# First heads, cap and constants loaded ahead of the branch; float64 conversion by 32-bit operations

## The chip, the core and the metric

The program runs on one core of a Trainium2 chip. Its engines are TensorE (PE, matmuls; PEld is its weight load), VectorE (DVE), ScalarE (ACT), GpSimd (POOL, unused here but for four memsets) and SyncE (SP), whose queue issues nearly all DMA transfers. The metric is device time in microseconds, the median of several runs.

## What is computed

Three layers, one after the other: attention with a soft cap, a feed-forward layer with a squared-ReLU-like function, and a second one with a maximum of three products. All tensors are float32 at the start; the weights reach the chip as float64 (see below).

```python
# 4 batches, 12 heads, 448 positions, head size 64; cap = 30
scores = q @ k.T / 8
scores = cap * tanh(scores / cap)
attn = exp(scores - max); attn /= attn.sum() + 1e-9
x = (attn @ v), heads side by side           # 1792 x 768
h = x @ w_in                                 # 768 -> 2048
g = where(h >= 1, h, where(h <= -1, 0, (h + 1)**2 / 4))
y = g @ w_out                                # 2048 -> 768
m = max(y @ w1, y @ w2, y @ w3)              # 768 -> 768, three times
out = m @ w_o2                               # 768 -> 768
```

## The kernel before

The entry (line 202) reads the cap's bits into a register on every engine and branches: above a limit it runs an arm that keeps the row maximum, otherwise (here) the arm without it. Each arm is the whole program, built by `softcap_attention_two_ffn` with its own pools.

**Work.** Activations lie transposed, channels on partitions, 448 positions of one batch along the free side. Batch 0 goes first: its attention, six pairs of heads, then the four matmul layers. Batch 1's attention is interleaved with batch 0's layers, batches 2 and 3's attention with batch 1's layers; the last two batches go through the layers together with a seven-product (Strassen) scheme. A matmul of the layers is three passes of float32r (a high and a low part of each operand), lines 863 to 865; the first six weight tiles (`PLAIN = 6`) are used as plain float32 matmuls, line 858, two passes of records each.

**Attention of a pair.** Two loads bring q and k of its two heads (`load_qk`, line 546), one brings v (549). Four chunks of keys: scores on TensorE (589 in batch 0, 578 later), tanh on ScalarE (596), exp (643). VectorE adds the four exps (281, tile `se`), TensorE sums over partitions with a tile of ones (672, 658), the sums go through memory to be inverted on few partitions (750, 771, 753, 758; the last pair inverts on VectorE at 782), and VectorE multiplies (281, tile `xf`) before the split into `x`.

**Weights.** On the first pass each weight tile, 128 partitions by 768 or 512 float64 numbers, is loaded into one of three `raw` buffers and turned into float32 in place, on the two 32-bit words of each number: the low word gives three rounding bits (`s0`, on VectorE at 410 or ScalarE at 408), the sign bit is put beside them (`sign`, 415, on VectorE), the high word is scaled as a float to move the exponent (`s1`, 422, ScalarE), and both are joined into the tile `wf` (`s3`, 426, VectorE), which is stored to memory for later passes. Before the change `s0` and `sign` write 16-bit quarters of the 64-bit number. There are 64 such tiles: 40 of 768, 24 of 512.

**Order.** Nothing is scheduled by the framework inside an arm. `Plan` gathers operations with a cost per engine, a due time (`want`) and the buffers that they take, plays them against each other at build time (`run`, line 65) and writes them out in the order of their planned starts; an operation with costs for two engines goes to the one that the plan finds free sooner. So a changed cost or dependency reorders the engines' instructions far from where it stands. On the chip each engine runs its list in order and waits on semaphores.

Of the kernel before, what the change touches and what calls it, by code (L numbers as in the profile page):

```python
# [10 lines left out]
I32 = mybir.dt.int32  # L11
U16 = mybir.dt.uint16
U32 = mybir.dt.uint32
BF16 = mybir.dt.bfloat16
# [9 lines left out]
class Plan:  # L24
# [29 lines left out]

    def op(self, cost, fn, want, deps=(), uses=(), takes=(), kind=None):
        o = Plan.Op()
        o.kind = kind
        o.cost, o.fn, o.want = cost, fn, want
        o.deps, o.takes = [d for d in deps if d is not None], list(takes)
        o.uses = list(dict.fromkeys([*uses, *takes]))  # L60
        for b in o.uses:
            b.users += 1
        for b in o.takes:
            self.order[b.pool].append((want, len(self.ops), b))
        o.n, o.out, o.t0, o.t1, o.e = 0, [], None, None, None
        self.ops.append(o)
        return o
# [133 lines left out]
def kernel(tc: tile.TileContext, qk, v, cap, *rest):  # L201


    bits = tc.nc.values_load(cap.bitcast(I32)[0:1, 0:1])
    with tc.If((bits & 0x7FFFFFFF) > LIMIT_BITS) as test:
        softcap_attention_two_ffn(tc, qk, v, cap, *rest, keep_max=True)
    with test.Else():
        softcap_attention_two_ffn(tc, qk, v, cap, *rest, keep_max=False)
# [3 lines left out]
def softcap_attention_two_ffn(  # L212
    ctx: ExitStack,
    tc: tile.TileContext,
    qk: bass.AP,
    v: bass.AP,
    cap: bass.AP,
# [34 lines left out]
    slots = {"u": 37, "h": 9, "v": 3, "w": 4, "wf": 4, "raw": 3, "rc": 2, "s": 2, "a": 1, "m": 3}  # L252
    const = pool("const", 1)
# [33 lines left out]
    def c_tt(n):  # L287
# [3 lines left out]


    ones = const.tile([C, D], F32, name="ones")
    nc.vector.memset(ones, 1.0)
    cap_sb = const.tile([P, 1], F32, name="cap_sb")
    nc.scalar.dma_start(out=cap_sb, in_=cap)

    nc.vector.scalar_tensor_tensor(
        out=cap_sb, in0=cap_sb, scalar=-1.0, in1=cap_sb, op0=ALU.mult, op1=ALU.max
    )  # L300
    qscale = const.tile([P, 1], F32, name="qscale")
    nc.vector.reciprocal(out=qscale, in_=cap_sb)
    nc.vector.tensor_scalar(
        out=qscale, in0=qscale, scalar1=1.0 / float(D) ** 0.5, scalar2=None, op0=ALU.mult
    )
# [79 lines left out]
    def fetch_first(i, want):  # L385
# [15 lines left out]
        def part(dtype, x):  # L401
            r = raw.tile.bitcast(dtype).rearrange("p (n four) -> p n four", four=4)
            return r[:, :n, x]

        def s0(e):
            lo, out_ = words()[0].bitcast(U32), part(U16, 0)
            if e == "A":
                nc.scalar.activation(out=out_, in_=lo, func=AF.Copy, scale=7.49 * 2.0**-32)  # L408
                return
            nc.vector.tensor_scalar(  # L410
                out=out_, in0=lo, scalar1=2.0**-29, scalar2=7.0, op0=ALU.mult, op1=ALU.min
            )

        def sign(e):
            nc.vector.tensor_scalar(  # L415
                out=part(U16, 1), in0=part(U16, 3), scalar1=0x8000, scalar2=None,
                op0=ALU.bitwise_and,
            )
# [20 lines left out]
        c = op({"D": 0.66 * k + 0.12}, sign, want - 17.7, [b], [raw])  # L439
# [88 lines left out]
    def attention(b, i, begin, last):  # L528
# [8 lines left out]
        qkt = [unit("qk")]  # L537
# [3 lines left out]

        def load_qk(e):
            for j in range(2):
                src = qk[b, 2 * i + j].rearrange("t p s -> p t s")
                o = slice(j * D, (j + 1) * D)
                nc.sync.dma_start(out=qkt[0].tile[o], in_=src[o])
# [6 lines left out]
        ql = op({"Q": 2.0}, load_qk, begin - (10 if full else 6), takes=qkt)  # L553
# [938 lines left out]
```

## Time and profile before

| | us |
|---|---|
| median of 3 runs | 996.36 (995.25 to 998.95) |
| profiled execution | 995.53 |
| its span, first to last instruction | 993.7 |
| TensorE busy | 963.0 (97%) |
| VectorE busy | 748.0 (75%) |
| ScalarE busy | 602.0 (61%) |
| DMA | 210.96 MB, mean 212 GB/s |

Busy times are sums over the whole span; the parts of the program have different limits, so they are read by stretches. Matmuls are pipelined and the profile models their ends, so small gaps between them do not show as idleness.

### The profile page before, as it was taken

The page shows a single profiled execution, that of the slowest core. Times are in us where ns is not written, and L with a number is a line of the kernel's source. Part 1 is how long each engine was busy: PE and PEld are TensorE (multiplying, and loading weights), DVE is VectorE, ACT ScalarE, POOL GpSimd, SP SyncE. Part 2 cuts the span into 40 slices and gives each one's busy share as a digit, 9 for nine tenths or more (in the row PEclk, how much of TensorE's full clock was granted, in tenths as well). Part 3 has the DMA queues.
Part 4 walks back from the last instruction along what each step waited for, and adds up shares of the span by engine and source line. Part 5 has one row for each costly group of instructions (what it writes and reads, how often), then busy time and mean ns, then how long its engine had stood idle before and what let it go on. Part 6 is the DMA issues. An engine that isn't in the chain of part 4 may idle for free.

```text
span 993.7 us, 14604 instructions
## 1 busy us (share of the span) xinstructions
PE 963.0 (97%) x5356; PEld 769.6 (77%) x5356; DVE 748.0 (75%) x1205; ACT 602.0 (61%) x876; POOL 0.2 (0%) x4
## 2 busy tenths in 40 slices
PE   5799999999999999999999999999999999999998
PEld 1124777877868877777777778999999999999997
DVE  1679999998989677877655667676898767858782
ACT  4788999787888478754445555555764524232431
POOL 0000000000000000000000000000000000000000
PEclk9799999999999999999999999999999999999999
DMA  5448877898898878688898765572364347437243
GB/s 127 150 147 261 264 230 226 266 292 274 289 293 270 293 248 277 224 283 286 289 319 275 228 209 188 166 238 80 129 200 139 107 147 235 136 103 238 88 147 131
DMA packets 111533, 210.96 MB, mean 212 GB/s; under 512 B 13022, under 2 KB 71518, under 8 KB 111454
## 3 DMA queue, kind: packets, MB, share of 16 engines
q1 hardware_dynamic: 109930, 209.87, 66.3%
q8 instruction: 44, 0.72, 0.3%
q10 hardware_dynamic: 1524, 0.08, 0.1%
q14 instruction: 35, 0.29, 0.1%
HBM read 142.90 MB, written 66.93 MB: 211 GB/s over the span
## 4 chain that ended last, share of the span: by engine, by line
PE 77%; ACT 9%; DVE 7%; DMA 4%; issue 2%; ACTq 0%; SPq 0%; DVEq 0%
PE ps_m L1263 21%; PE ps_s L1263 11%; PE ps_m L863 9%; PE ps_m L865 8%; PE ps_m L864 8%; PE ps_a L798 6%; PE ps_a L1263 5%; PE ps_s L578 4%; ACT raw L408 3%; PE ps_m L858 3%; DVE raw L415 2%; ACT t L643 2%; ACT raw L422 1%; DVE wf L426 1%; PE ps_s L589 1%
## 5 line engine op out<-in xcount | busy, mean ns | idle before, releaser
L1263 PE MATMUL ps_m<-op,w 128*128 128x448 f32 x1008 | 212.2, 368 | 0.0
L1263 PEld LDWEIGHTS ps_m<-op,w 128*128 128x128 f32 x1008 | 189.2, 188 | 19.1
L281 DVE TENSOR_TENSOR w<-wf,w 128x768 fp32r<-128x768 f32 (+1 forms) x146 | 120.6, 828 | 9.8 <-ACT w L276 8.0
L596 ACT ACTIVATE t<-ps_s,qscale 112x896 f32<-112x896 f32 x96 | 92.5, 1002 | 45.8 <-PE ps_s L578 39.2
L1263 PE MATMUL ps_s<-op,w 128*128 128x448 f32 x522 | 112.2, 368 | 0.0
L1263 PEld LDWEIGHTS ps_s<-op,w 128*128 128x128 f32 x522 | 98.0, 188 | 9.9
L643 ACT ACTIVATE t<-t,cap_sb 112x896 f32<-112x896 f32 x96 | 96.0, 1039 | 4.8 <-DVE rs L730 3.0
L276 ACT ACTIVATE w<-wf 128x768 fp32r<-128x768 f32 (+1 forms) x86 | 64.4, 750 | 55.9 <-PE ps_m L865 34.3
L798 PE MATMUL ps_a<-t,v 112*32 112x448 f32 (+1 forms) x752 | 82.8, 564 | 3.0 <-DVE xf L281 1.5
L863 PE MATMUL ps_m<-y,w 128*128 128x448 f32 x216 | 80.6, 373 | 0.0
L865 PE MATMUL ps_m<-y,w 128*128 128x448 f32 x216 | 79.2, 367 | 0.8 <-DVE w L281 0.8
L864 PE MATMUL ps_m<-y,w 128*128 128x448 f32 x216 | 79.0, 366 | 0.0
L278 DVE CAST w<-wf 128x512 fp32r<-128x512 f32 (+1 forms) x60 | 29.5, 492 | 57.3 <-PE ps_m L865 44.2
L863 PE MATMUL ps_m<-g,w 128*128 128x448 f32 x192 | 71.8, 374 | 0.0
L865 PE MATMUL ps_m<-g,w 128*128 128x448 f32 x192 | 70.5, 367 | 1.4 <-DVE w L281 1.4
L864 PE MATMUL ps_m<-g,w 128*128 128x448 f32 x192 | 70.3, 366 | 0.0
L422 ACT ACTIVATE raw<-raw 128x768 f32<-128x768 f32 (+1 forms) x64 | 53.6, 839 | 27.5 <-DVE raw L415 22.9
L415 DVE TENSOR_SCALAR raw<-raw 128x768 uint16<-128x768 uint16 (+1 forms) x64 | 60.1, 938 | 11.8 <-ACT raw L408 10.8
L408 ACT ACTIVATE raw<-raw 128x768 uint16<-128x768 uint32 (+1 forms) x37 | 62.9, 1700 | 2.2 <-DMA raw<-in_w_out 1.0
L281 DVE TENSOR_TENSOR w<-ss,w 128x384 fp32r<-128x384 f32 x80 | 43.7, 555 | 24.9 <-ACT w L276 22.8
L798 PEld LDWEIGHTS ps_a<-t,v 112*32 112x32 f32 (+1 forms) x752 | 24.2, 114 | 48.6 <-issue 32.8
L276 ACT ACTIVATE w<-ss 128x384 fp32r<-128x384 f32 x69 | 35.3, 520 | 40.8 <-PE ps_m L1263 21.0
(140 smaller groups left out, 1730.4 us busy)
## 6 DMA issues: line engine op xcount, KB each, us to landing
p<-w SPq DMA_DIRECT2D x60, 384.0 KB
w<-p SPq DMA_DIRECT2D x60, 384.0 KB
w<-wf SPq DMA_DIRECT2D x40, 384.0 KB
wf<-w SPq DMA_DIRECT2D x40, 384.0 KB
wf<-w SPq DMA_DIRECT2D x80, 192.0 KB
raw<-in_w SPq DMA_DIRECT2D x18, 768.0 KB
raw<-in_w_in SPq DMA_DIRECT2D x16, 768.0 KB
raw<-in_w_out SPq DMA_DIRECT2D x24, 512.0 KB
```

The source lines that it names most:

```text
L276: nc.scalar.activation(out=out_, in_=in_, func=AF.Copy)
L281: nc.vector.tensor_tensor(out=out_, in0=a, in1=b, op=o)
L408: nc.scalar.activation(out=out_, in_=lo, func=AF.Copy, scale=7.49 * 2.0**-32)
L415: nc.vector.tensor_scalar(out=part(U16, 1), in0=part(U16, 3), scalar1=0x8000, scalar2=None, op0=ALU.bitwise_and,)
L422: nc.scalar.activation(out=hi, in_=hi, func=AF.Copy, scale=2.0**-112)
L596: nc.scalar.activation(out=t[c].tile, in_=ps.tile[:C, :, :S], func=AF.Tanh, scale=qscale[:C])
L643: lambda e, c=c: nc.scalar.activation(out=t[c].tile, in_=t[c].tile, func=AF.Exp, scale=cap_sb[:C]),
L798: nc.tensor.matmul(pa.tile[j * D + d : j * D + d + n, :S], vt.tile[:, j, c, d : d + n], t[c].tile[:, j], start=start, stop=stop,)
L863: nc.tensor.matmul(ps.tile[:, :S], wh, a.tile[:, 0], start=start, stop=False)
L864: nc.tensor.matmul(ps.tile[:, :S], wh, a.tile[:, 1], start=False, stop=False)
L865: nc.tensor.matmul(ps.tile[:, :S], wl, a.tile[:, 0], start=False, stop=stop)
L1263: nc.tensor.matmul(get(), w_, x_, start=start and z == 0, stop=stop and z == 2, skip_group_check=begun,)
```

## The change

Ahead of the branch the entry now opens a pool, loads the first pair's q and k into a tile of its own (`qk0`), loads the cap, fills the ones, and works out the cap's absolute value and the scale of the scores; both arms use them. The first pair's scores then depend on no planned load. The pool of `u` buffers has 36 instead of 37 slots. In the conversion `s0` writes the whole low word as a 32-bit integer, and `sign` takes the sign bit from the high word and joins it to the low word in one operation with two inputs, at a planned cost of 1.05 instead of 0.66 us per 1000 columns.

```diff
+    def fixed(self, tile_):
+        b = Plan.Buf(None, None)
+        b.tile = tile_
+        return b
...
-        o.uses = list(dict.fromkeys([*uses, *takes]))
+        o.uses = [b for b in dict.fromkeys([*uses, *takes]) if b.pool]
...
-def tile_softcap_attention_two_ffn_kernel(tc: tile.TileContext, qk, v, cap, *rest):
-    bits = tc.nc.values_load(cap.bitcast(I32)[0:1, 0:1])
+@with_exitstack
+def tile_softcap_attention_two_ffn_kernel(
+    ctx: ExitStack, tc: tile.TileContext, qk, v, cap, *rest
+):
+
+
+    nc = tc.nc
+    bits = nc.values_load(cap.bitcast(I32)[0:1, 0:1])
+    const = ctx.enter_context(tc.tile_pool(name="const", bufs=1))
+    qk0 = const.tile([128, 2, qk.shape[4]], F32, name="qk0")
+    load_heads(nc, qk0, qk, 0, 0)
+    cap_sb = const.tile([128, 1], F32, name="cap_sb")
+    nc.scalar.dma_start(out=cap_sb, in_=cap)
+    ones = const.tile([v.shape[2], 64], F32, name="ones")
+    nc.vector.memset(ones, 1.0)
+    nc.vector.scalar_tensor_tensor(
+        out=cap_sb, in0=cap_sb, scalar=-1.0, in1=cap_sb, op0=ALU.mult, op1=ALU.max
+    )
+    qscale = const.tile([128, 1], F32, name="qscale")
+    nc.vector.reciprocal(out=qscale, in_=cap_sb)
+    nc.vector.tensor_scalar(
+        out=qscale, in0=qscale, scalar1=0.125, scalar2=None, op0=ALU.mult
+    )
+    consts = const, qk0, cap_sb, ones, qscale
     with tc.If((bits & 0x7FFFFFFF) > LIMIT_BITS) as test:
-        softcap_attention_two_ffn(tc, qk, v, cap, *rest, keep_max=True)
+        softcap_attention_two_ffn(tc, consts, qk, v, *rest, keep_max=True)
     with test.Else():
-        softcap_attention_two_ffn(tc, qk, v, cap, *rest, keep_max=False)
+        softcap_attention_two_ffn(tc, consts, qk, v, *rest, keep_max=False)
+
+
+def load_heads(nc, to, qk, b, i):
+    D = qk.shape[3] // 2
+    for j in range(2):
+        src = qk[b, 2 * i + j].rearrange("t p s -> p t s")
+        o = slice(j * D, (j + 1) * D)
+        nc.sync.dma_start(out=to[o], in_=src[o])
...
-    slots = {"u": 37, "h": 9, "v": 3, "w": 4, "wf": 4, "raw": 3, "rc": 2, "s": 2, "a": 1, "m": 3}
-    const = pool("const", 1)
+    slots = {"u": 36, "h": 9, "v": 3, "w": 4, "wf": 4, "raw": 3, "rc": 2, "s": 2, "a": 1, "m": 3}
+    const, qk0, cap_sb, ones, qscale = consts
...
-    ones = const.tile([C, D], F32, name="ones")
-    nc.vector.memset(ones, 1.0)
-    cap_sb = const.tile([P, 1], F32, name="cap_sb")
-    nc.scalar.dma_start(out=cap_sb, in_=cap)
-    nc.vector.scalar_tensor_tensor(
-        out=cap_sb, in0=cap_sb, scalar=-1.0, in1=cap_sb, op0=ALU.mult, op1=ALU.max
-    )
-    qscale = const.tile([P, 1], F32, name="qscale")
-    nc.vector.reciprocal(out=qscale, in_=cap_sb)
-    nc.vector.tensor_scalar(
-        out=qscale, in0=qscale, scalar1=1.0 / float(D) ** 0.5, scalar2=None, op0=ALU.mult
-    )
...
         def s0(e):
-            lo, out_ = words()[0].bitcast(U32), part(U16, 0)
+            lo = words()[0]
             if e == "A":
-                nc.scalar.activation(out=out_, in_=lo, func=AF.Copy, scale=7.49 * 2.0**-32)
+                nc.scalar.activation(
+                    out=lo, in_=lo.bitcast(U32), func=AF.Copy, scale=7.49 * 2.0**-32
+                )
                 return
             nc.vector.tensor_scalar(
-                out=out_, in0=lo, scalar1=2.0**-29, scalar2=7.0, op0=ALU.mult, op1=ALU.min
+                out=lo, in0=lo.bitcast(U32), scalar1=2.0**-29, scalar2=7.0,
+                op0=ALU.mult, op1=ALU.min,
             )
 
         def sign(e):
-            nc.vector.tensor_scalar(
-                out=part(U16, 1), in0=part(U16, 3), scalar1=0x8000, scalar2=None,
-                op0=ALU.bitwise_and,
+            lo, hi = words()
+            nc.vector.scalar_tensor_tensor(
+                out=lo, in0=hi, scalar=-(2**31), in1=lo, op0=ALU.bitwise_and,
+                op1=ALU.bitwise_or,
             )
...
-        c = op({"D": 0.66 * k + 0.12}, sign, want - 17.7, [b], [raw])
+        c = op({"D": 1.05 * k + 0.15}, sign, want - 17.7, [b], [raw])
...
-        qkt = [unit("qk")]
+        early = first and i == 0
+        qkt = [plan.fixed(qk0) if early else unit("qk")]
...
-        def load_qk(e):
-            for j in range(2):
-                src = qk[b, 2 * i + j].rearrange("t p s -> p t s")
-                o = slice(j * D, (j + 1) * D)
-                nc.sync.dma_start(out=qkt[0].tile[o], in_=src[o])
...
-        ql = op({"Q": 2.0}, load_qk, begin - (10 if full else 6), takes=qkt)
+        ql = None if early else op(
+            {"Q": 2.0}, lambda e: load_heads(nc, qkt[0].tile, qk, b, i),
+            begin - (10 if full else 6), takes=qkt,
+        )
```

**SyncE at the program's start**, through the branch to the first loads of the arm. Before:

```order
L1488 UNCONDITIONAL_BRANCH
L204 TENSOR_LOAD in_cap_ptr
L204 TENSOR_LOAD in_cap
L205 REGISTER_ALU
L205 COMPARE_AND_BRANCH
L546 DMA qk<-in_qk 64x2x448 x2
L549 DMA v<-in_v 112x2x256
L546 DMA qk<-in_qk 64x2x448 x2
```

Now:

```order
L1502 UNCONDITIONAL_BRANCH
L239 DMA qk_65<-in_qk 64x2x448 x2
L211 TENSOR_LOAD in_cap_ptr
L211 TENSOR_LOAD in_cap
L228 REGISTER_ALU
L228 COMPARE_AND_BRANCH
L560 DMA v<-in_v 112x2x256
L239 DMA qk<-in_qk 64x2x448 x2
```

The two loads of the first heads (`qk`, now `qk_65`) moved from behind the branch to the head of the queue; what follows the branch stands as it did, without them.

**VectorE in the first pairs' attention**, from behind the sum of the first pair on; `rs<-ps_r` is such a sum, `rc` is the inversion of a pair's sums, `xf` the product with them, `raw` the conversion of weights. Before:

```order
L281 TENSOR_TENSOR se<-t 112x896
L281 TENSOR_TENSOR se<-se,t 112x896
L771 RECIPROCAL rc<-rc 56x16
L281 TENSOR_TENSOR se<-se,t 112x896
L730 TENSOR_SCALAR rs<-ps_r,eps_sb 128x224
L410 TENSOR_SCALAR raw<-raw 128x768
L415 TENSOR_SCALAR raw<-raw 128x768
L281 TENSOR_TENSOR se<-t 112x896
L281 TENSOR_TENSOR se<-se,t 112x896
L771 RECIPROCAL rc<-rc 56x16
L410 TENSOR_SCALAR raw<-raw 128x768
L281 TENSOR_TENSOR xf<-ps_a,rs 128x448
```

Now:

```order
L312 TENSOR_TENSOR se<-t 112x896
L785 RECIPROCAL rc<-rc 56x16
L312 TENSOR_TENSOR se<-se,t 112x896 x2
L744 TENSOR_SCALAR rs<-ps_r,eps_sb 128x224
L312 TENSOR_TENSOR se<-t 112x896
L312 TENSOR_TENSOR xf<-ps_a,rs 128x448
L312 TENSOR_TENSOR se<-se,t 112x896
L309 CAST x<-xf 128x448
L312 TENSOR_TENSOR x<-xf,x 128x448
L785 RECIPROCAL rc<-rc 56x16
L312 TENSOR_TENSOR se<-se,t 112x896
```

The first `xf` moved ahead of all conversion and of the second pair's `rc`; it stood behind three conversion steps and that `rc`.

**VectorE at the end of batch 0's attention**, from the last pair's first sum on; `wf` are the joined weights that the plain matmuls read, `rs` with x4 the last pair's inversion. Before:

```order
L281 TENSOR_TENSOR se<-t 112x896
L281 TENSOR_TENSOR xf<-ps_a,rs 128x448
L426 SCALAR_TENSOR_TENSOR wf<-raw 128x768
L278 CAST x<-xf 128x448
L281 TENSOR_TENSOR x<-xf,x 128x448
L771 RECIPROCAL rc<-rc 56x16
L281 TENSOR_TENSOR se<-se,t 112x896 x2
L426 SCALAR_TENSOR_TENSOR wf<-raw 128x768 x2
L281 TENSOR_TENSOR qk_lo<-qk,qk_hi 128x896
L782 RECIPROCAL rs<-rs 128x112 x4
L281 TENSOR_TENSOR xf<-ps_a,rs 128x448
```

Now:

```order
L312 TENSOR_TENSOR se<-t 112x896
L312 TENSOR_TENSOR se<-se,t 112x896
L785 RECIPROCAL rc<-rc 56x16
L312 TENSOR_TENSOR se<-se,t 112x896
L312 TENSOR_TENSOR xf<-ps_a,rs 128x448
L442 SCALAR_TENSOR_TENSOR wf<-raw 128x768
L309 CAST x<-xf 128x448
L312 TENSOR_TENSOR x<-xf,x 128x448
L796 RECIPROCAL rs<-rs 128x112 x4
L312 TENSOR_TENSOR xf<-ps_a,rs 128x448
L442 SCALAR_TENSOR_TENSOR wf<-raw 128x768
L312 TENSOR_TENSOR x<-xf,x 128x448
```

Here the second of the four first `wf` stood ahead of the last sums, with one more much earlier; now the first of them stands behind the last sum, and the second behind the four reciprocals. (In the same place the three exponent steps of ScalarE, line 422, now 438, stand behind its last exp.)

## Rows read from the trace of the kernel before

**Rows 1.** Three stretches: us, busy PE PEld DVE ACT POOL, granted clock, DMA share, GB/s

```profile
25.00:50.00 25.00, 19.11 (x160) 4.60 (x160) 15.85 (x22) 17.57 (x19) 0.00 (x0) 0.80 0.48 149
81.00:330.00 249.00, 241.93 (x1327) 188.36 (x1327) 232.84 (x335) 212.85 (x264) 0.00 (x0) 1.00 0.86 267
330.00:600.00 270.00, 270.00 (x1675) 212.82 (x1675) 181.89 (x276) 159.56 (x215) 0.00 (x0) 1.00 0.80 263
```

**Rows 2.** Chain of waits, 0 to 50 us: start us, us, what

```profile
0.72 0.86 SPq L204
...
2.24 2.53 issue
4.77 6.23 DMA qk<-in_qk
...
41.41 0.45 DVE xf L281
```

**Rows 3.** Timeline of the start: start us, us, engine line operation [idle before]

```profile
4.77 3.17 SPq L546 DMA_DIRECT2D qk<-in_qk  x2
...
11.52 1.28 ACT L325 ACT_TABLE_LOAD   x1 [11.52 <-DVE cap_sb L298]
...
14.06 1.01 ACT L596 ACTIVATE t<-ps_s,qscale 112x896 f32<-112x896 f32 x1 [1.05 <-PE ps_s L589]
...
19.36 1.09 DVE L281 TENSOR_TENSOR se<-t 112x896 f32<-112x896 f32 x1 [6.16 <-ACT t L643]
```

**Rows 4.** Timeline of ScalarE, later in batch 0's attention

```profile
47.00 0.93 ACT L422 ACTIVATE raw<-raw 128x768 f32<-128x768 f32 x1 [3.66 <-DVE rs L730]
...
67.19 1.26 ACT L422 ACTIVATE raw<-raw 128x768 f32<-128x768 f32 x1
...
71.34 1.04 ACT L643 ACTIVATE t<-t,cap_sb 112x896 f32<-112x896 f32 x1
```

**Rows 5.** Timeline of VectorE, end of batch 0's attention

```profile
69.73 0.39 DVE L278 CAST x<-xf 128x448 fp32r<-128x448 f32 x1
...
76.21 2.99 DVE L782 RECIPROCAL rs<-rs 128x112 f32<-128x112 f32 x4
...
79.30 0.62 DVE L281 TENSOR_TENSOR xf<-ps_a,rs 128x448 f32<-128x448 f32 x1
```

**Rows 6.** Chain of waits, where the plain matmuls begin

```profile
77.25 1.41 PE ps_s L578 x12
...
81.00 22.75 PE ps_m L858 x60
```

**Rows 7.** Conversion steps by line and shape: xcount | busy, mean ns | idle before

```profile
L415 DVE TENSOR_SCALAR raw<-raw 128x768 uint16<-128x768 uint16 x40 | 41.9, 1048 | 7.5 <-ACT raw L408 7.0
L408 ACT ACTIVATE raw<-raw 128x768 uint16<-128x768 uint32 x21 | 41.1, 1955 | 1.1 <-ACT rs L728 0.6 <-DMA raw<-in_w 0.5
...
L426 DVE SCALAR_TENSOR_TENSOR wf<-raw 128x768 int32<-128x768 int32 x40 | 38.4, 963 | 1.5 <-ACT raw L422 1.5
L422 ACT ACTIVATE raw<-raw 128x768 f32<-128x768 f32 x40 | 37.2, 932 | 20.5 <-DVE raw L415 16.6 <-DVE rs L730 3.7
...
L408 ACT ACTIVATE raw<-raw 128x512 uint16<-128x512 uint32 x16 | 21.9, 1366 | 1.1 <-DMA raw<-in_w_out 1.0
...
L410 DVE TENSOR_SCALAR raw<-raw 128x768 uint16<-128x768 uint32 x19 | 19.9, 1046 | 0.3 <-DMA raw<-in_w_in 0.3
...
L422 ACT ACTIVATE raw<-raw 128x512 f32<-128x512 f32 x24 | 16.4, 683 | 7.0 <-DVE raw L415 6.3 <-ACT t L596 0.5
```

**Rows 8.** Waits from 81 to 330 us: total us, times, longest

```profile
ACT raw L422 <- DVE raw L415: 22.9, 32, 2.2
...
PE ps_m L865 <- DVE w L281: 2.2, 4, 0.8
```

**Rows 9.** SyncE's queue: two of the loads of raw weight tiles

```profile
76.71 0.43 SPq L399 DMA_DIRECT2D raw<-in_w_in  x1
...
106.69 0.33 SPq L399 DMA_DIRECT2D raw<-in_w_in  x1
```

More of the change, by code (lines that the diff above doesn't have):

```diff
@@ L11 @@
 I32 = mybir.dt.int32
-U16 = mybir.dt.uint16
 U32 = mybir.dt.uint32
-BF16 = mybir.dt.bfloat16
 I64 = mybir.dt.int64
@@ L198, in emit, with kernel @@
             o.fn(o.e)
-def kernel(tc: tile.TileContext, qk, v, cap, *rest):
-    bits = tc.nc.values_load(cap.bitcast(I32)[0:1, 0:1])
+@with_exitstack
+def kernel(
+    ctx: ExitStack, tc: tile.TileContext, qk, v, cap, *rest
[18 more added lines that the diff above has]
+    consts = const, qk0, cap_sb, ones, qscale
     with tc.If((bits & 0x7FFFFFFF) > LIMIT_BITS) as test:
-        softcap_attention_two_ffn(tc, qk, v, cap, *rest, keep_max=True)
+        softcap_attention_two_ffn(tc, consts, qk, v, *rest, keep_max=True)
     with test.Else():
-        softcap_attention_two_ffn(tc, qk, v, cap, *rest, keep_max=False)
+        softcap_attention_two_ffn(tc, consts, qk, v, *rest, keep_max=False)
[5 more added lines that the diff above has]
+        nc.sync.dma_start(out=to[o], in_=src[o])
 @with_exitstack
@@ L214, in softcap_attention_two_ffn @@
     tc: tile.TileContext,
+    consts,
     qk: bass.AP,
     v: bass.AP,
-    cap: bass.AP,
     w_in: bass.AP,
@@ L399, in load @@
             nc.sync.dma_start(out=raw.tile[:, :n], in_=units[i])
-        def part(dtype, x):
-            r = raw.tile.bitcast(dtype).rearrange("p (n four) -> p n four", four=4)
-            return r[:, :n, x]
         def s0(e):
-            lo, out_ = words()[0].bitcast(U32), part(U16, 0)
+            lo = words()[0]
             if e == "A":
-                nc.scalar.activation(out=out_, in_=lo, func=AF.Copy, scale=7.49 * 2.0**-32)
+                nc.scalar.activation(
+                    out=lo, in_=lo.bitcast(U32), func=AF.Copy, scale=7.49 * 2.0**-32
+                )
                 return
             nc.vector.tensor_scalar(
-                out=out_, in0=lo, scalar1=2.0**-29, scalar2=7.0, op0=ALU.mult, op1=ALU.min
+                out=lo, in0=lo.bitcast(U32), scalar1=2.0**-29, scalar2=7.0,
+                op0=ALU.mult, op1=ALU.min,
             )
         def sign(e):
-            nc.vector.tensor_scalar(
-                out=part(U16, 1), in0=part(U16, 3), scalar1=0x8000, scalar2=None,
-                op0=ALU.bitwise_and,
+            lo, hi = words()
+            nc.vector.scalar_tensor_tensor(
+                out=lo, in0=hi, scalar=-(2**31), in1=lo, op0=ALU.bitwise_and,
+                op1=ALU.bitwise_or,
             )
```

## The prediction

> **What bounds the kernel now.** I read the stretches first, then the chain of waits, and last the timelines of the places where TensorE stands. TensorE is busy in nearly all of the span, so the question is where it is not. From 330 to 600 us it is busy all of the time [rows 1], and after the first pass over the weights the built order of its matmuls is the same in both programs but for a few that change places; nothing that this change does can be worth much there. Two places are left. The **head**, 0 to 81 us, is the first batch's attention: TensorE works 19.1 us of the 25 between 25 and 50, at a granted clock of 0.80 [rows 1], because tanh and exp on ScalarE are the slower side. The **first pass over the weights**, 81 to 330 us, has TensorE idle for only 7.07 us of 249, beside a VectorE at 232.8 us (94%), a ScalarE at 212.9 us (85%) and transfers at 0.86 [rows 1]. All four are near their limit there, and the float64 conversion that the change touches runs only in that stretch and at the end of the head. So the most that I see is 7 us in the stretch, some more that pipelined ends hide, and what the head gives.
>
> **The loads outside of the arms.** SyncE spends 0.72 to 2.24 us on reading the cap and branching, then 2.53 us until its first instruction in the arm, and only at 4.77 us issues the first heads, which land at 11.00 [rows 2]. In the new order that issue stands ahead of the reading, so it moves to 0.72: 4.05 us earlier, with landing near 6.95. The reading and the branch now follow the two issues, which take 3.17 us of SyncE's queue [rows 3]: 0.72 + 3.17, and then the same 4.05 us to the arm, make 7.94, just when SyncE was through with the first heads before (4.77 + 3.17). So everything behind them in that queue, the second pair's heads first, is issued when it was; nothing of it is earlier. The cap constants: ScalarE's issue moves up by the same step; before, the table load that waits for the cap ran from 11.52 to 12.80 and the first tanh started at 14.06 [rows 3]. Shifted, the load ends at 8.75, the first tanh can start at 10.0, and the scores are last there, as before. VectorE now waits for the cap (until about 7.5) ahead of its branch; behind that wait stand its own reading and branch, 4.05 us more on SyncE, and its first sum, at 19.36 before [rows 3], is not due before 15. I take 4.05 us for the first tanh; bounds 2.5, were the issue no earlier than the old branch at 2.24, and 4.8, were it at the span's start.
>
> **The head, reordered.** The planner's order of the head is new, and this counts for more than the shift. Before, VectorE did a low-word step, a sign step and the wait for the second reciprocal ahead of the first product with the reciprocal, xf; it came at 41.41, and the chain of waits runs through it to TensorE [rows 2]. In the new order xf stands ahead of all conversion. Before, ScalarE did two exponent steps (L422, 0.93 and 1.26 us) between the tanhs, one of them after 3.66 us of idleness; the last exp ended at 72.38 [rows 4]. In the new order all three exponent steps stand behind the last exp. So the last exp comes 4.05 + 2.2 = 6.2 us earlier, at 66.1. Bounds: 68.3 where only the shift is left, 62.4 where the 3.66 of idleness goes too [rows 4].
>
> But what stood between the tanhs now stands behind them. From the last exp VectorE has in row: sum 1.09, xf 0.62, first weights 0.95, cast 0.39, difference 0.62, four reciprocals 2.99, xf 0.62, second weights 0.95, difference 0.62, third weights 0.95, xf 0.62: 10.4 us (durations of [rows 3, 5, 7]; a difference is taken as xf, the same shape). TensorE can start the plain matmuls 2.8 us after the exp, does four, stands 1.6 us for the xf behind the reciprocals, and has 13 done at 14.4 us after the last exp, none of the next batch's 24 scores. A plain one takes 0.755 us here (30 in 22.75 us, two records each) [rows 6]. Before, 8.6 us after the last exp (81.0) it had 6 done and the 24 scores, which are 2.8 us at 1.41 for twelve [rows 6]. Seven plain ones more are 5.3 us, so the new order is where the old one was at 14.4 - 5.3 + 2.8 = 11.9 us instead of 8.6: **3.3 us given back**. The head is then 6.2 - 3.3 = 2.9 us ahead; bounds 6.6 ahead (last exp at 62.4) and 0.8 (68.3).
>
> **The 32-bit steps.** By the built order the low-word step goes to ScalarE 26 times wide and 19 narrow (before 21 and 16), to VectorE 14 and 5 (before 19 and 8). The step on ScalarE takes 1955 ns wide and 1366 narrow; the exponent step, the same engine and shape with the same stride, 32 bits in and out, takes 932 and 683 [rows 7]. Nothing in the trace parts the 16-bit output from the reading of unsigned integers. I take the output as the cause: the ratio holds for both widths, so the cost is by the element, and VectorE's two 16-bit forms (1046 and 1048) are both slower than its 32-bit form with two inputs (963) [rows 7]. With that, ScalarE goes from 62.9 to 26 x 0.932 + 19 x 0.683 = 37.2 us, **25.7 us less**; at the old price it would be 76.8, 13.9 more. Those are the bounds. The Trainium skill, "ScalarE: Activation LUTs", section "What ACT_TABLE_LOAD costs", gives 186 ns + 0.833 ns an element for an activation with immediate scale, for fp32 and bf16 alike: an estimate of 826 ns wide. By that rule a 2-byte output costs nothing, the excess would lie in something that the change keeps, and the change would add work to ScalarE; the trace disagrees with its number already (932, 1955), and no run shown tells which half of it fails.
>
> VectorE: the sign step becomes the form of L426, 963 for 1048 ns, 40 times, and narrow ones likewise: 5 us less. The low-word step, 8 fewer: 7.5 us less at 1046 ns. Together **12.5 us less** of 232.8. The page "VectorE: DVE Perf Modes" of the Trainium skill, section "What auto-detection actually checks", lets a one-source operation in SBUF run two elements a cycle; the 16-bit step at 1046 ns does not show it. If the 32-bit step did, another 8 us or so would go.
>
> In the stretch a raw tile comes back every third load: 76.71 to 106.69 is six loads, 5.0 us each [rows 9]. The largest wait there is inside the conversion, 22.9 us of ScalarE for the sign step [rows 8]. Taking about 1.0 us out of a tile's way on ScalarE, and 38 us of work off the two engines that TensorE waits for (2.2 us for weights' low parts alone [rows 8]), should free all of the 7.07 us that TensorE stands. I take 7.1; bounds 0 and 10, where the hidden gaps go as well. What is late next is TensorE itself. The tile qk0 costs one of 37 slots for the whole program; after 330 us TensorE has no idle time in which this would show, so I take nothing.
>
> **Sum.** The profiled execution took 995.53 us (span 993.7 and 1.8 around it). 995.5 - 2.9 - 7.1 = 985.5. The median of the runs shown is 0.83 above that execution, so 986.3.
>
> **Rivals.**
> *More of it goes.* The last exp at 62.4 and the hidden gaps too: 995.5 - 6.6 - 10 + 0.8 = 979.7. For it: the idle pieces of ScalarE in the head stand where the order is new. Against it: the queue of reciprocals through memory stays.
> *The low-word step keeps its price on ScalarE*, since reading unsigned integers is what costs. Then ScalarE gains 13.9 us of work in a stretch where it is at 85%, VectorE is rid of 12.5, and the two cancel: 995.5 - 2.9 + 0.8 = 993.4, from 990 to 999. By the ScalarE page of the Trainium skill, as told above, it would be this one.
> *Weights come too late (slower).* No raw tile comes back before the last exp, so the fourth load, issued before while the attention ran, waits until then. Where the last exp comes at 68.3, the head gains 0.8 us, but the stream of weights is one tile behind, 5.0 us [rows 9], and TensorE stands in front of the plain matmuls; if its granted clock then falls as it did between 25 and 50 (0.80 in the mean, so 10 of the 25 us at 1.2 GHz instead of 2.4 [rows 1]), that is 5.0 more: 995.5 - 0.8 + 5 + 5 + 0.8 = 1005.5. It decides from a last exp at 69.1 on (72.4 - 3.3), where the head has nothing left to pay for it, and only if the stretch gains nothing.
>
> **How the numbers follow.** Chances: the forecast 0.55, more of it 0.18, the old price 0.18, late weights 0.09. A measurement of this kernel tells about 0.5% (5 us) from no change, so faster means under 991.4. The forecast's own spread (981 to 993) lies under that about nine times in ten; with the first rival, and a quarter of the second, that makes 0.72 faster; 0.19 the same; 0.09 slower. The range goes from 979 to 997: it leaves out the slow rival, the far end of the second and a little of the first.
>
> **What would show it.** Right: the first heads issued at about 0.7 us and the first tanh near 10; the last exp near 66, the last plain matmul near 101, as against 103.75; the low-word step on ScalarE near 0.93 us, the sign step near 0.96; TensorE idle under 2 us between 81 and 330. Wrong: a low-word step still near 1.9 us; a last exp at 68 or later; TensorE standing for first weights after the attention, at a lower granted clock.

## The result, and the profile after

The changed kernel takes 982.65 us in the median of four runs (980.67 to 983.78), the kernel before 995.81 beside it: a ratio of 0.9865, 95% interval 0.983 to 0.9899. The forecast was 986.3, from 979 to 997. The profiled execution took 983.78 us with a span of 982.0, 11.7 less than before.

Four stretches of the kernel after, with the columns of [rows 1]:

```profile
25.00:50.00 25.00, 21.78 (x184) 4.89 (x176) 16.72 (x25) 19.53 (x21) 0.00 (x0) 0.86 0.53 172
130.00:140.00 10.00, 8.01 (x32) 6.91 (x31) 10.00 (x16) 9.94 (x17) 0.00 (x0) 0.83 0.71 221
81.00:330.00 249.00, 247.01 (x1378) 198.92 (x1379) 220.15 (x325) 193.48 (x277) 0.00 (x0) 0.99 0.89 280
330.00:600.00 270.00, 270.00 (x1678) 212.76 (x1677) 186.09 (x282) 165.54 (x222) 0.00 (x0) 1.00 0.80 259
```

TensorE's idle time between 81 and 330 us fell from 7.07 to 1.99 us, all of it between 130 and 140, where the granted clock also is 0.83 in the mean. VectorE and ScalarE are 12.7 and 19.4 us less busy there.

The chain of waits of the kernel after, the start and the plain matmuls (against [rows 2, 6]):

```profile
0.73 3.58 DMA qk<-in_qk
4.31 2.87 issue
7.17 3.31 PE ps_s L603 x12
...
71.35 7.21 PE ps_m L872 x18
...
82.33 16.73 PE ps_m L872 x44
```

The heads are there at 4.31 us, at 11.00 before. What is last for the first scores is no longer a transfer but 2.87 us in which TensorE waits for nothing that the profile shows; I take them for its way into the arm. The last plain matmul ends at 82.33 + 16.73 = 99.06, at 103.75 before. Behind that matmul TensorE has the same work left in both programs: the same 508 matmuls lie up to it in the traces of all kernels of this study, among themselves differently arranged. So the 11.7 us split cleanly: **4.7 ahead of it, and 7.0 behind it** (993.7 - 103.75 = 889.95 before; 982.0 - 99.06 = 882.94 after).

The start and the end of the first attention in the timeline of the kernel after (against [rows 3, 4]):

```profile
0.73 1.42 SPq L239 DMA_DIRECT2D qk<-in_qk  x2
...
6.08 1.28 ACT L341 ACT_TABLE_LOAD   x1 [6.08 <-issue]
...
9.01 1.01 ACT L610 ACTIVATE t<-ps_s,qscale 112x896 f32<-112x896 f32 x1 [1.43 <-PE ps_s L603]
...
14.30 1.09 DVE L312 TENSOR_TENSOR se<-t 112x896 f32<-112x896 f32 x1 [6.38 <-ACT t L657]
...
63.14 1.04 ACT L657 ACTIVATE t<-t,cap_sb 112x896 f32<-112x896 f32 x1
64.08 2.52 ACT L438 ACTIVATE raw<-raw 128x768 f32<-128x768 f32 x3
...
66.76 3.27 PE L872 MATMUL ps_m<-xf,wf 128*128 128x448 f32 x8 [0.34 <-DVE wf L442]
71.35 7.21 PE L872 MATMUL ps_m<-xf,wf 128*128 128x448 f32 x18 [1.32 <-DVE xf L312]
```

The conversion steps of the kernel after by line and shape (against [rows 7]; L420 and L424 are the low-word step, L431 the sign step):

```profile
L431 DVE SCALAR_TENSOR_TENSOR raw<-raw 128x768 int32<-128x768 int32 x40 | 38.4, 961 | 7.0 <-ACT raw L420 6.6
...
L420 ACT ACTIVATE raw<-raw 128x768 int32<-128x768 uint32 x26 | 23.8, 914 | 6.9 <-DMA raw<-in_w 4.5 <-DMA raw<-in_w_in 1.8 <-ACT rs L742 0.6
...
L420 ACT ACTIVATE raw<-raw 128x512 int32<-128x512 uint32 x19 | 12.8, 672 | 2.6 <-DMA raw<-in_w_out 2.6
...
L424 DVE TENSOR_SCALAR raw<-raw 128x768 int32<-128x768 uint32 x14 | 8.1, 578 | 0.4 <-DMA raw<-in_w 0.2
```

The step on ScalarE still reads unsigned integers and writes 32 bits: 914 for 1955 ns, 672 for 1366. On VectorE it fell too, from 1046 to 578. The waits from 81 to 330 us of the kernel after (against [rows 8]):

```profile
ACT raw L438 <- DVE raw L431: 5.1, 9, 1.6
ACT raw L420 <- DMA raw<-in_w: 4.5, 6, 1.3
...
PE ps_m L877 <- ACT h L307: 2.0, 1, 2.0
```

The wait inside the conversion is down from 22.9 us to 5.1; ScalarE now waits for weights to land, and TensorE waits once, 2.0 us, for an eviction.

### The profile page after: what moved, and what is told of

Same layout as the page of the kernel before. It is cut to its first block, busy times and chain, and to the rows that moved or that the text cites. A ratio compares the mean times of both kernels' runs of the same rounds, so it can differ in the third digit from the quotient of the medians.

```text
span 982.0 us, 14606 instructions
## 1 busy us (share of the span) xinstructions
PE 959.8 (98%) x5356; PEld 771.0 (79%) x5356; DVE 730.1 (74%) x1191; ACT 582.8 (59%) x890; POOL 0.2 (0%) x4
## 4 chain that ended last, share of the span: by engine, by line
PE 94%; ACT 4%; DVE 1%; issue 1%; DMA 0%; ACTq 0%; DVEq 0%
PE ps_m L1277 21%; PE ps_m L877 14%; PE ps_m L878 13%; PE ps_m L879 13%; PE ps_s L1277 11%; PE ps_a L812 7%; PE ps_s L592 5%; PE ps_a L1277 5%; PE ps_m L872 3%; ACT t L657 2%; PE ps_r L686 1%; PE ps_s L603 1%; ACT t L610 1%; DMA qk<-in_qk 0%; DVE rs L796 0%
## 5 line engine op out<-in xcount | busy, mean ns | idle before, releaser
L307 ACT ACTIVATE w<-wf 128x768 fp32r<-128x768 f32 (+1 forms) x90 | 67.2, 747 | 57.4 <-PE ps_m L879 31.5
L309 DVE CAST w<-wf 128x512 fp32r<-128x512 f32 (+1 forms) x56 | 27.0, 482 | 60.2 <-PE ps_m L879 43.8
L877 PE MATMUL ps_m<-x,w 128*128 128x448 f32 x156 | 59.3, 380 | 2.0 <-ACT h L307 2.0
L431 DVE SCALAR_TENSOR_TENSOR raw<-raw 128x768 int32<-128x768 int32 (+1 forms) x64 | 54.9, 858 | 7.9 <-ACT raw L420 7.5
L878 PE MATMUL ps_m<-x,w 128*128 128x448 f32 x156 | 57.6, 370 | 0.0
```

Source lines behind the costliest of these rows:

```text
L307: nc.scalar.activation(out=out_, in_=in_, func=AF.Copy)
L431: nc.vector.scalar_tensor_tensor(out=lo, in0=hi, scalar=-(2**31), in1=lo, op0=ALU.bitwise_and, op1=ALU.bitwise_or,)
L877: nc.tensor.matmul(ps.tile[:, :S], wh, a.tile[:, 0], start=start, stop=False)
L878: nc.tensor.matmul(ps.tile[:, :S], wh, a.tile[:, 1], start=False, stop=False)
```

## Experiments

For each kernel the table gives the timed median, the ratio to the runs of before on the same chip, and from its trace the end of the last plain matmul and what was left of the span behind it. The last two columns come from one execution each. The kernels ran on several chips, on which before has medians from 994.89 to 996.73, so medians of different chips are to be compared by the ratio. loads_only, bits_only, order_kept_16 and sign_16 share one chip; shift_only, bits_old_cost, act32_dve16 and dve32_act16 a second; loads_old_cost and v_banks_old a third; v_banks and exp_dve a fourth.

| kernel | median us | ratio, 95% interval | last plain ends | behind it |
|---|---|---|---|---|
| before | 995.81 | | 103.75 | 889.95 |
| after | 982.65 | 0.9865 (0.983 to 0.9899) | 99.06 | 882.94 |
| loads_only | 992.19 | 0.9963 (0.9947 to 0.9978) | 98.64 | 890.8 |
| bits_only | 988.36 | 0.9911 (0.9884 to 0.9939) | 103.83 | 882.9 |
| bits_old_cost | 984.80 | 0.9888 (0.9868 to 0.9907) | 105.82 | 880.0 |
| order_kept_16 | 986.81 | 0.9893 (0.9862 to 0.9923) | 99.90 | 890.9 |
| act32_dve16 | 983.87 | 0.9884 (0.9864 to 0.9904) | 96.44 | 882.9 |
| dve32_act16 | 986.86 | 0.9919 (0.9901 to 0.9937) | 98.44 | 879.5 |
| sign_16 | 982.02 | 0.986 (0.9836 to 0.9884) | 96.50 | 882.7 |
| shift_only | 984.81 | 0.9888 (0.9866 to 0.991) | 100.26 | 883.0 |
| loads_old_cost | 982.95 | 0.9868 (0.9837 to 0.9899) | 99.95 | 882.2 |
| v_banks | 979.45 | 0.983 (0.9806 to 0.9855) | 94.17 | 881.0 |
| v_banks_old | 979.70 | 0.9826 (0.9801 to 0.9851) | 96.84 | 879.5 |
| exp_dve | 976.17 | 0.9798 (0.978 to 0.9817) | 94.65 | 878.8 |

### One part of the change at a time

loads_only is the kernel after with the steps of before:

```
-            lo = words()[0]
+            lo, out_ = words()[0].bitcast(U32), part(U16, 0)
...
-        c = op({"D": 1.05 * k + 0.15}, sign, want - 17.7, [b], [raw])
+        c = op({"D": 0.66 * k + 0.12}, sign, want - 17.7, [b], [raw])
```

> The kernel before with the first heads, the cap and the constants loaded ahead of the branch (36 slots of u), the conversion left with its 16-bit forms. Theory (two gains that add): the head gains what it gained in the kernel after, last exp near 64 us and last plain matmul near 99 to 100, while TensorE still stands for about 7 us between 81 and 330 us: 995.8 - 4.7 = 991. Rival (the head's lead is eaten by the stretch, since the weights arrive no sooner): last plain matmul near 99, but more idle time of TensorE behind it, 995 to 996. Second rival (the stretch stands only because the head is late): 984.

bits_only is the kernel before with the changed steps, the mirror of that diff, and the loads inside the arms.

> The kernel before with the low-word and sign steps in 32 bits and the planner's new cost for the sign step, all loads inside the arms (37 slots of u). Theory: head as before (first tanh near 14.1, last exp near 72), low-word step on ScalarE 0.91 us and on VectorE 0.58 us, TensorE idle under 2.5 us between 81 and 330 us: 995.8 - 7 = 989, from 987 to 991. Rival (the gain of the stretch needs the earlier head): 994 to 996.

Both came as the first theory said: loads_only moves the last plain matmul to 98.64 and leaves 890.8 us behind it (TensorE stands for 9.4 us between 81 and 330, where about 7 were expected); bits_only leaves it at 103.83 and has 882.9 behind it. The parts add, to within the scatter: 3.7 us and 7.6 us by the medians, 11.3 together, and 13.2 for both.

### Price or order

The steps' forms change their price, and the planner's new cost of the sign step changes the order. bits_old_cost has the new forms in the order of before, word for word on TensorE and SyncE:

```
-        c = op({"D": 1.05 * k + 0.15}, sign, want - 17.7, [b], [raw])
+        c = op({"D": 0.66 * k + 0.12}, sign, want - 17.7, [b], [raw])
```

> The kernel before with the low-word and sign steps in 32 bits and nothing else: the planner keeps the old costs, so that the order of every engine is that of before, and the low-word step stays with the engine that had it (ScalarE 21 wide and 16 narrow, VectorE 19 and 8). Theory (the price of the step frees the stretch): from the last plain matmul (near 104) to the end 883 us as in bits_only, not 890 as before: 988 to 989. Rival (the gain is from the order that the sign step's new planned cost brings): 993 to 996.

order_kept_16 is the other way round: the order of after with the 16-bit forms.

> The kernel after with its order of every engine unchanged, but the low-word and sign steps in their 16-bit forms. Theory (the price of the step is what the stretch gains from): 26 wide and 19 narrow low-word steps at 1.955 and 1.366 us put about 40 us back on ScalarE, VectorE gets 11 back, TensorE stands 7 us or more between 81 and 330 us: 991 to 996. Rival (the new order of the stretch is the gain, the prices do not matter): 983.

Three kernels then split the price in the order of after. sign_16 has the sign step alone in 16 bits. From it, act32_dve16 puts VectorE's low-word step back to 16-bit output, and dve32_act16 ScalarE's:

```
-                    out=lo, in_=lo.bitcast(U32), func=AF.Copy, scale=7.49 * 2.0**-32
+                    out=part(U16, 0), in_=lo.bitcast(U32), func=AF.Copy, scale=7.49 * 2.0**-32
```

> The kernel after, its order unchanged, with the sign step alone back in its 16-bit form. Theory: the sign step goes from 0.96 to 1.05 us, 40 times, 3.4 us more on VectorE, which is off the path now: 983 to 984, not to be told from the kernel after. Rival (the wait for the sign step, the largest of ScalarE there, sets the stretch): a few us of TensorE's idle time come back, 985 to 988.

> The run sign_16 (order of after, low-word step in 32 bits, 982.0 us) with VectorE's share of the low-word step back in 16-bit output: 14 wide and 5 narrow steps at 1.05 in place of 0.58 us, some 8 us more on VectorE. Theory (ScalarE's price is what counts, 40 us against 8): 883 to 885 us behind the last plain matmul, 982 to 984. Rival (VectorE at 94% of the stretch is the one that holds TensorE): 887 to 890 behind it, 986 to 989.

> The run sign_16 (order of after, low-word step in 32 bits, 982.0 us) with ScalarE's share of the low-word step back in 16-bit output: 26 wide and 19 narrow steps at 1.955 and 1.366 in place of 0.91 and 0.67 us, 40 us more on ScalarE. Theory (ScalarE's price is what counts): 888 to 891 us behind the last plain matmul, 986 to 990. Rival (VectorE's share is what counts, ScalarE has room at 78%): 883 to 885 behind it, 982 to 984.

The stretch from 81 to 330 us with the columns of [rows 1]. bits_old_cost:

```profile
81.00:330.00 249.00, 249.00 (x1379) 197.62 (x1378) 228.85 (x344) 188.74 (x270) 0.00 (x0) 1.00 0.90 278
```

order_kept_16:

```profile
81.00:330.00 249.00, 241.38 (x1336) 190.37 (x1336) 223.02 (x321) 226.58 (x275) 0.00 (x0) 0.99 0.88 272
```

In the order of before the new forms alone free all of TensorE's visible idle time; 880.0 us are left behind the last plain matmul, 10 less than before, and the median is 1.1% lower (0.9 to 1.3), more than the theory had. (The traced span fell by 7.9 us, since the head of that execution ended 2.1 us later.) The rival, that the order gains, is out here, because this kernel has the order of before on every engine. order_kept_16 shows the same from the other side in its trace: TensorE stands 7.6 us again, and 890.9 are left. Its timed runs lie between 980.6 and 992.5, though, the traced one being the slowest, and their median, 986.81, lies between its theory and its rival. So by the medians the price is worth 4 to 5 us in the order of after (982.65, or 982.02 of sign_16 on the same chip), and by the traces 8. I can't say which is nearer.

With the 16-bit forms the rival is not out. order_kept_16 and loads_only differ in the planned cost of the sign step alone and ran on one chip: 986.81 and 992.19, so the new order would be worth 5.4 us there by the medians, while their traces have the same left behind the last plain matmul (890.9 and 890.8). Price and order thus don't simply add, and why the timed runs and the traces part here is open.

The sign step is worth nothing that could be told (882.7 left behind, 982.02). The forms of the low-word step in dve32_act16, by line and shape (ScalarE in 16 bits, VectorE in 32):

```profile
L425 ACT ACTIVATE raw<-raw 128x768 uint16<-128x768 uint32 x26 | 50.9, 1957 | 1.3 <-ACT rs L746 0.6 <-DMA raw<-in_w 0.3 <-DMA raw<-in_w_in 0.2
...
L429 DVE TENSOR_SCALAR raw<-raw 128x768 int32<-128x768 uint32 x14 | 8.1, 576 | 0.0
```

and in act32_dve16:

```profile
L425 ACT ACTIVATE raw<-raw 128x768 int32<-128x768 uint32 x26 | 23.9, 920 | 4.3 <-DMA raw<-in_w 3.4 <-ACT rs L746 0.6
...
L429 DVE TENSOR_SCALAR raw<-raw 128x768 uint16<-128x768 uint32 x14 | 14.5, 1034 | 0.1
```

The input is the same in all four; the price goes with the output. Its width and its stride change together here, and no run parts them. With ScalarE in 32 bits VectorE's form changes nothing that could be told (882.9 and 882.7 left behind, overlapping intervals). With ScalarE in 16 bits the median is 986.86: 3.0 above act32_dve16 on the same chip, and by the ratios 0.6% above sign_16, with intervals that don't touch. The traced execution of dve32_act16, 979.71, seems to contradict this, but it is the one trace in which TensorE's last stage ran at another pitch. One run of 72 matmuls there, first in dve32_act16 and then in sign_16 (start us, us):

```profile
718.41 14.76 PE L1281 MATMUL ps_m<-op,w 128*128 128x448 f32 x72
```

```profile
714.60 15.04 PE L1281 MATMUL ps_m<-op,w 128*128 128x448 f32 x72
```

0.28 us in 72; from its first matmul to the last of this form the stage takes 352.37 us there and 359.14 in each of the other thirteen traces, 6.8 us more. At the usual pitch 886.2 would be left behind, and the time would be 986.5, as in the other six timed runs (985.8 to 989.0). So ScalarE's price counts. That VectorE's counts too while ScalarE's is the old one is what the traces say (886.2 against 890.9 for order_kept_16), but not the medians (986.86 and 986.81): it is not shown.

### The planned cost of the sign step

bits_only took 988.36 us and bits_old_cost 984.80; they differ in the planned cost alone. They ran on two chips; by the ratios that is 2.3 us, with overlapping intervals, and by the traces 2.9 us behind the last plain matmul. In the kernel after TensorE stands 2.0 us near 132 us (bits_only has the like, 2.3 us between 130 and 180), and the lower clock of those 10 us, 0.83, costs up to 1.7 more, an estimate from 0.17 of 10 us. loads_old_cost is the kernel after with the old cost.

> The kernel after with the planner's old cost of the sign step (0.66 us per 1000 elements + 0.12 in place of 1.05 + 0.15), so that the order of every engine is that of loads_only and the steps are in 32 bits. From the last plain matmul's start to the first matmul of the last two layers' stage loads_only took 523.0 us, the kernel after 514.8, the order of before with 32-bit steps 511.4. Theory (the new planned cost gives 3.4 us of the stretch back through one stall near 132 us and the lower clock behind it): last plain matmul near 98.5, 511 to 512 in the stretch, 979 to 980.5. Rival (the stall belongs to the earlier head, whatever the planned cost): 514 to 515, 982 to 984.

It took 982.95 us, as the kernel after: the theory is out. Its trace shows the standing a little later (us, busy PE PEld DVE ACT POOL, clock, DMA, GB/s):

```profile
140.00:150.00 10.00, 8.11 (x63) 4.98 (x65) 10.00 (x16) 9.25 (x18) 0.00 (x0) 1.00 0.86 253
```

VectorE is busy for the whole of those 10 us, as it is from 130 to 140 in the kernel after. That alone doesn't make TensorE stand: v_banks_old, below, has VectorE busy from 130 to 140 just the same, and TensorE too. What TensorE waits for depends on the order: an eviction on ScalarE in the kernel after (`h`, 2.0 us), a sum of the attention on VectorE in bits_only (`se`, 2.3), a weight and such a sum on VectorE in loads_old_cost (`w`, 0.9, and `se`, 0.8). The old cost gains 2.9 us behind the last plain matmul in the traces of one pair (882.9 and 880.0), 0.7 in another (882.9 and 882.2) and 1.5 in a third (v_banks and v_banks_old, 881.0 and 879.5); in none of the three do the timed runs tell it from nothing. Which rule would place the work well is open.

### The head

shift_only moves the first heads out of the arm, but lets the planner place everything as if they were loaded inside:

```
-        ql = None if early else op(
-            {"Q": 2.0}, lambda e: load_heads(nc, qkt[0].tile, qk, b, i),
-            begin - (10 if full else 6), takes=qkt,
+        ql = op(
+            {"Q": 2.0},
+            lambda e: None if early else load_heads(nc, qkt[0].tile, qk, b, i),
+            begin - (10 if full else 6), takes=[] if early else qkt,
```

> The kernel after, with its loads ahead of the branch, but planned as if the first heads were loaded inside the arm: TensorE's order is word for word that of the run bits_only (last exp 72.0 us, last plain matmul 103.8, 988.4 us), so only the start moves. Theory (the shift of 5 us carries through, and the head's new order is worth nothing in sum, because what it gains by the last exp it gives back before the plain matmuls): first tanh near 9, last exp near 67, last plain matmul near 99, 983 to 984, as the kernel after. Rival (the shift is eaten by the reciprocals' way through memory, and the new order is what gains): last plain matmul at 101 to 103, 986 to 988.

First tanh 9.26, last exp 68.43, last plain matmul 100.26: of the 5 us of the shift 3.6 arrive in the marks (103.83 in bits_only); by the ratios of the timed runs it is 2.3, with overlapping intervals. The head's new order is worth 0.4 to 3.8 us more in the traces: five kernels with the order of after end their plain matmuls between 96.44 and 99.90. The timed runs of shift_only and the kernel after don't part the two (ratios 0.9888 and 0.9865, overlapping). Neither theory holds alone.

Those five have one order; besides the forms of their steps they differ by the granted clock. TensorE stands 2.6 us in all of them, near 31 us, for the first product with the reciprocal (xf), and then has 32 matmuls of the product with v in a row; what clock it gets for them differs. The kernel after:

```profile
33.03 6.20 PE L812 MATMUL ps_a<-t,v 112*32 112x448 f32 x32 [2.58 <-DVE xf L312]
```

sign_16, and its clock in that stretch (columns as in [rows 1]):

```profile
32.57 3.21 PE L816 MATMUL ps_a<-t,v 112*32 112x448 f32 x32 [2.58 <-DVE xf L313]
```

```profile
25.00:50.00 25.00, 19.58 (x188) 4.51 (x184) 17.87 (x27) 21.78 (x24) 0.00 (x0) 1.00 0.56 179
```

The same 32 matmuls take 6.20 us in the one and 3.21 in the other, half the clock and the whole (from 30 to 40 us it is 0.66 in the mean in the kernel after and 1.00 in sign_16), and ScalarE waits for what stands behind them: its last exp ends at 64.18 and at 61.65. v_banks_old takes the standing away. TensorE waits there because the third pair's product with v wants the one bank of the first; it now gets another:

```
-        pa = buf("m" if first and i % 2 else "a", "ps_a", [P, 512])
+        pa = buf("m" if first and i % 3 else "a", "ps_a", [P, 512])
```

> The run loads_old_cost with another PSUM bank for the third pair's product with v in the first batch (banks m for every pair whose number is no multiple of three, in place of the odd ones), so that it need not wait for the first product with the reciprocal. Theory (TensorE's 2.6 us of standing near 31 us and the 16 slow score products behind it, at half the clock, cost the head 2.5 to 4 us): TensorE without an idle time of over 1 us between 20 and 50 us, granted clock 1.00 there, last exp at 60 to 62, last plain matmul at 95 to 97, 976 to 978. Rival (ScalarE sets the head anyway, and the reciprocals' way through memory stands before the next pair instead): last exp at 63 to 65, 979 to 981.

> The kernel after with the bank change of v_banks_old alone, planned with the new cost of the sign step. Theory (the bank change is what gains, about 3 us of the head, whatever the planned cost): granted clock 1.00 from 25 to 50 us, last plain matmul's start at 95 to 97, 979 to 981. Rival (the head gains only together with the old planned cost): 982 to 984.

The slow matmuls behind the standing are the 32 products with v shown above; the first of these two texts calls them 16 score products, and those run at the whole clock in the trace of after. v_banks_old, 25 to 75 us:

```profile
25.00:50.00 25.00, 22.25 (x212) 4.81 (x208) 17.70 (x26) 21.64 (x24) 0.00 (x0) 1.00 0.59 179
50.00:75.00 25.00, 19.90 (x98) 7.27 (x92) 20.72 (x31) 16.55 (x22) 0.00 (x0) 0.93 0.48 170
```

The clock is 1.00 from 25 to 50 us, the longest standing left between 20 and 50 us is 1.09 us, the last exp ends at 59.95, the plain matmuls at 96.84. The marks are the theory's, or nearly; the time is the rival's, some 2 us above what the theory had. The median is 979.70, with every run (978.2 to 980.3) below the fastest of loads_old_cost on the same chip (981.4); the mean granted clock is 0.996 to 0.998 in its timed runs and 0.989 to 0.997 in those of loads_old_cost. v_banks has 979.45 (ratio 0.983, the kernel after 0.9865): the bank gains about 3 us under either planned cost. Left is the end of the head. exp_dve puts the exponent step of the first six weight tiles on VectorE:

```
-        d = op({"A": 1.0 * k + 0.19}, s1, want - 17.5, [c], [raw])
+        d = op({"D": 0.66 * k + 0.12} if i < PLAIN else {"A": 1.0 * k + 0.19}, s1, ...
```

> The run v_banks_old (979.7 us, last exp 59.95, last plain matmul's start 96.3) with the exponent step of the first six weight tiles on VectorE in place of ScalarE. Theory (behind the last exp TensorE stands for first weights, because their exponent steps come after it on ScalarE: 2 us before the plain matmuls and the low-clock stretch from 60 to 70): the first products of the conversion and the first plain weights are ready before the last exp, TensorE is fed from then on with the next batch's scores and plain matmuls, last plain matmul at 92 to 95, 976 to 978.5. Rival (the last pair's four reciprocals and xf are what comes last, the weights are not missing): last plain matmul at 96 to 97, 979 to 981.

TensorE's first plain matmuls in v_banks_old:

```profile
64.62 9.48 PE L872 MATMUL ps_m<-xf,wf 128*128 128x448 f32 x20 [0.72 <-ACT rs L742]
```

exp_dve, TensorE's timeline at the same place and two stretches:

```profile
63.10 0.97 PE L677 MATMUL ps_r<-se,ones 112*64 112x448 f32 x4 [1.50 <-DVE se L312]
...
65.73 4.78 PE L877 MATMUL ps_m<-xf,wf 128*128 128x448 f32 x12
```

```profile
50.00:75.00 25.00, 20.46 (x117) 7.80 (x109) 24.71 (x38) 19.40 (x24) 0.00 (x0) 1.00 0.56 175
81.00:330.00 249.00, 249.00 (x1407) 201.59 (x1406) 224.12 (x340) 178.95 (x255) 0.00 (x0) 1.00 0.87 282
```

20 matmuls in 9.48 us there, 12 in 4.78 here; the clock is 1.00 all through (in v_banks_old 0.83 from 60 to 70 us), the plain matmuls end at 94.65, and between 81 and 330 us TensorE doesn't stand at all. 976.17 us is 2.0% below before (1.8 to 2.2) and 6.5 below the kernel after: the best of the study. Marks and time are as the theory had them, but that first weights were missing is not shown. The trace of v_banks_old has no wait for one there: TensorE stands 1.95 us for the sum `se` and 0.72 for `rs`. And v_banks, with the exponent steps on ScalarE, ends its plain matmuls at 94.17.

## Why the prediction held, step by step

- **First tanh: mis-sized by 1.0 us.** Forecast near 10, measured 9.01. I moved the rows of before by 4.05 us as they stood. But the two issues take 1.42 us at the start, not 3.17, and the landing 3.58 from the issue, not 6.23; the claim that SyncE enters the arm "when it was" fell with that (the first load of v is issued at 6.66 us, 7.99 before). The scores then wait for 2.87 us in which the profile shows no wait, and not for the heads, which I had not looked for.
- **Last exp: mis-sized by 1.9 us**, 64.18 for 66.1 and inside the bounds (62.4 to 68.3). 1.0 of it is the start; the other 0.9 is not accounted for. It may be luck: between the traces of the five kernels with one order this mark lies from 61.6 to 65.0, and the two earliest have the highest granted clock from 25 to 50 us (1.00 and 0.93, against 0.86). That the work behind the last exp costs something was right: 8.2 us of lead at the last exp became 4.7 at the last plain matmul, so 3.5 went back, 3.3 forecast. The way was right too: the plain matmuls start 2.6 us after the last exp (forecast 2.8), four are done, TensorE stands 1.32 us for `xf` (1.6), and 13 are done 14.4 us after the last exp (14.4), as the rows at 66.76 and 71.35 show, ahead of the next batch's scores.
- **The head: 4.7 us for 2.9**, the term that was too small, since the gain by the last exp was.
- **Low-word step on ScalarE: right**, 0.914 us for about 0.93. The output was the cause and not the reading of unsigned integers, since the reading stayed. The second rival fell with it. The ScalarE page of the Trainium skill ("ScalarE: Activation LUTs", "What ACT_TABLE_LOAD costs") has one rate for fp32 and bf16; the 32-bit form here lies 11% above it (914 against an estimate of 826 from its figures), and no row of it covers an integer output on every fourth 16-bit place, which took 1955.
- **Sign step: right in size** (961 ns for 963), and worth nothing.
- **Low-word step on VectorE: left out of the sum**, 578 ns for 1046. "VectorE: DVE Perf Modes" of the Trainium skill, "What auto-detection actually checks", allows two elements a cycle for one source and a destination in SBUF with even counts. The two forms of the step part there: between 512 and 768 columns the 32-bit form takes 0.60 ns a column (424 and 578 ns), and the 16-bit form of act32_dve16, which the rule would let run as fast, 1.09 (755 and 1034). The term would have changed nothing that could be told: act32_dve16.
- **The stretch: 7.0 us for 7.1**, but by luck, since two errors cancel. The idle time fell to 1.99, as forecast, so that 5.1 of the 7.07 us came back, and not all of it as in the sum; the rest came from gaps that the view does not show. More of those was to be had: bits_old_cost gained 10.0, the upper bound I had set for hidden gaps. And the kernel after loses 2.0 us by one wait and up to 1.7 (the estimate above) by the clock behind it, between 130 and 140 us, in an order that I had taken to be neutral there. Of the 38 us of work taken off the two engines it was ScalarE's low-word step that counted in the order of after.
- **The slow rival** needed a last exp at 69.1; it came at 64.2, and TensorE stood 0.34 us for a first weight.
- Beside the terms, the profiled execution of before lay 0.83 us under its median, that of after 1.13 above: 2.0 of the 3.7 us between 986.3 and 982.65.

## What to carry to other kernels

Price a conversion step by the width and stride of what it writes, by engine, from the same kernel's rows; where two engines are near full, their relief can give more than the visible idle time of a third (10.0 us for 7.07 here). Take one fixed piece of work that all variants have done by the same point (here the last plain matmul) and split every difference there: it kept a head effect of 5 us and a stretch effect of 7 apart where the totals of one kernel scattered by 2 to 12. One trace can still be an odd one, so set it beside the timed runs. Where TensorE stands 2 us, count also what a lower clock may take from the matmuls behind it, and look for the buffer whose single copy makes it stand.

## What the runs showed of the hardware

- A 16-bit output on every fourth 16-bit place cost ScalarE 1955 ns for 768 elements against 914 with 32-bit output on every second word, and VectorE 1046 against 578, the input being the same. Whether it is the width or the stride is open.
- Two head loads issued at the very start took 1.42 us of SyncE's queue, those in the arm of before 3.17; the heads had landed 3.58 us after the first issue began, 6.23 before.
- After the same 2.58 us of standing the same 32 matmuls ran at half the clock in one kernel (6.20 us) and at the whole in another (3.21 us).
- In one of fourteen traces the last stage's matmuls came 2% closer (14.76 us for 72 instead of 15.04), 6.8 us in all, with nothing in the program that would tell it from its neighbours. Why is open, and so is how much of the scatter of other timed runs is this.
